# Sums of q and k's seven products kept in PSUM, and the last pair of tiles by seven products too

## The chip, the cores and the metric

The kernel runs on one NeuronCore of a Trainium2 chip. The metric is the device time of one execution in microseconds (us); lower is better. The engines named below are TensorE (PE, matmuls; its weight loads are PEld), VectorE (DVE), ScalarE (ACT), GpSimd (POOL) and SyncE (SP, whose queue issues most DMAs). PSUM is the memory that matmuls write; it has eight banks of 512 float32 columns for each partition, and GpSimd doesn't read it.

## What is computed

One transformer-like block on x of 2048 rows and 512 columns, in float32: a layer norm, then a sliding dilated attention beside a feed-forward with squared ReLU, whose SiLU gates the attention's output.

```python
xn = _layernorm(x, axis=-1)
s = _A_ref(xn, A_wqkv, A_wo)      # 32 heads of 16; each row attends to 8 rows, 2 apart
g = _silu(_B_ref(xn, B_w1, B_b1, B_w2, B_b2))
return x + s * g

# in _A_ref
qkv = (x @ wqkv).reshape(B, S, 3, H, Dh)
...
# in _B_ref, F = 1792
h = x @ w1 + b1
h = where(h > 0, h, 0) ** 2
out = h @ w2 + b2
```

## The kernel before

**Precision.** Each matmul operand is split into a high part (rounded to the type that TensorE multiplies fast) and a low part (the rest). A product of two operands is three passes: high by high, high by low, low by high (`PASSES`). One matmul is 128 x 128 by 128 x 512 and fills a bank. `split` makes both parts: ScalarE copies the high one, VectorE or GpSimd subtracts for the low one.

**Stage one** (`px`, `pstg`, `pxT` pools): the 2048 rows are 16 tiles of 128, handled in pairs (a, a + 1). For each tile, q, k and v come from xn times three 512 x 512 weights, 12 matmuls each (four pieces of 128 of the contraction, three passes; `qkv`). ScalarE evacuates each bank into a staging tile `stg` (four buffers), which is stored to HBM in the layout of the attention (`store_qkv`, in SP's queue), from where it is loaded again, unit by unit, by DMAs that ScalarE issues (`load_u`).

A pair can be done in two ways. `pair` does six `qkv`, 72 matmuls. `pair_of_seven` treats the q and k of a pair as a 2 x 2 block product: the two tiles by the two halves of the contraction, times the two halves of the weights of q (Q0, Q1) and of k (K0, K1). It takes seven products of six matmuls in place of eight (the form of Strassen's scheme due to Winograd), 42 matmuls and 24 for v. With sums S of x's quarters (made by `copy_quarter`, `sums`, `high_sums`, `low_sums` beside the pair before) and sums T1 to T4 of the weights:

- P1 = x(a, half 0) Q0, P2 = x(a, half 1) Q1, P5 = S1 T1, P6 = S2 T2, P7 = S3 T3, P3 = S4 K1, P4 = x(b, half 1) T4
- U2 = P1 + P6, U3 = U2 + P7
- q of a = P1 + P2; k of a = U2 + P5 + P3; q of b = U3 + P4; k of b = U3 + P5

Before, `SEVEN` holds the pairs 4, 6, 8, 10 and 12; pairs 0, 2 and 14 are plain. Each product goes to a bank of its own (`psA`, four banks in rotation, of which v's products take theirs too). ScalarE copies P1 and P5 into q's and k's staging tiles; VectorE does five additions of 128 x 512, each reading a bank, and GpSimd two.

**The order** is written by hand. `Ordered` keeps every engine's instructions in program order. `beside(a, step)` is called at six points of each pair and runs what `plan` puts there for the next pairs (transposes, splits of x, the sums S, layer norms, shuffles), takes in feed-forward weights (`next_w`, where `ahead` says so), and calls `pump`, which lets VectorE's attention work run on as far as a planned clock allows: `clock["V"]` to at most `LATE` = 3000 ns past `clock["PE"]`. `not_before` sets VectorE's planned clock to when an input is due.

**Stage two**: four chunks of 512 rows, each with 14 slices of the feed-forward (`up`, 12 matmuls into `psH`, then ScalarE and GpSimd; `down`, 12 matmuls into four banks of `psA`), the attention's output product, and the gate. Slices 0 and 1 of the first chunk are computed within pair 14, as `last`.

**Weights' homes**: the split weights of qkv and the sums T1 to T4 fill ten buffers, of which `HOME` says which feed-forward slice takes which buffer over once the old content is used. There are 14 slices; slices 0 to 4 are split during stage one, at steps (10, 2), (12, 4), (14, 0), (14, 2) and (14, 4).

The records of the trace have the line of a helper (L87) for every engine instruction, so groups are told apart by tile names: `pm` the products of a seven-product pair, `pq` the plain ones, `ph` and `pb` the feed-forward's up and down, `S` and `Sf` the sums of x.

Of the kernel before, what the change touches and what calls it, by code (L numbers as in the profile page):

```python
# [8 lines left out]
F32 = mybir.dt.float32  # L9
# [5 lines left out]
P = 128  # L15
# [25 lines left out]
HOME = {0: 10, 1: T1, 2: T2, 3: T3, 4: T4, 5: Q0, 6: Q1, 7: K0, 8: K1, 9: V0, 10: V1}  # L41

SEVEN = range(4, 14, 2)
# [14 lines left out]
def body(ctx: ExitStack, tc: tile.TileContext, x, wqkv, wo, w1, b1, w2, b2, out):  # L58
# [52 lines left out]
    def psA(name):  # L111
        return psum.tile([P, 512], F32, name=name, tag="acc", bufs=4)
# [421 lines left out]
    def product(a, n, lhs, w):  # L534

        ps = psA(f"pm{a}_{n}")
        k = 0
        for i in range(2):
            for p, q in PASSES:
                PE.matmul(ps, lhs(p, i), wq[w][:, q, i, :], start=k == 0, stop=k == 5)  # L540
                k += 1
        return ps.rearrange("p (g c) -> p g c", g=GR)
# [4 lines left out]
    def qkv(t, s, between=None, late=False):  # L547
# [5 lines left out]
        for n, (kt, a, b) in enumerate(order):  # L553
            PE.matmul(ps, xt[t][:, a, kt], wq[2 * s + kt // 2][:, b, kt % 2, :], start=n == 0, stop=n == 11)
            if between and n == 5:
                between()
# [196 lines left out]
    def pair_of_seven(a):  # L753
# [39 lines left out]
        qkv(b, 2)  # L793
# [213 lines left out]
```

## Time and profile before

| | |
|---|---|
| median of three runs | 496.27 us (492.69 to 496.73) |
| span of the profiled execution, first to last instruction | 487.2 us |
| matmuls and transposes on TensorE | 2124 |
| ScalarE, GpSimd busy | 220.0 us, 242.7 us |
| stage one, from the first matmul on x to the first `up` | 6.92 to 127.00 us |

The time of a run is that of the whole execution on the device. The span counts from the first to the last instruction of the program; what lies around it is the difference, some 9 us between the median and the span of the profiled execution.

In the rows below, a row of the timeline reads: start us, length us, engine, line, operation, out<-in, shapes, count, and in brackets the engine's idle time before it and what ended that. A row of the groups reads: line, engine, operation, out<-in, shapes, count, then busy us, mean ns of one, idle time before them and what ended it. A row of the chain reads: start us, length us, what. A row of the stretches reads: from:to, length, then busy us (and instructions) of PE, PEld, DVE, ACT and POOL, the granted clock, the DMA share and GB/s. The slices are 40 equal parts of the span, each digit the busy share in tenths, 9 for 90% or more.

### The profile page before, as it was taken

The numbers are of one execution on the slowest core, as the hardware profiler recorded it, in microseconds if no ns is written. First come the engines' busy times: TensorE is split into PE (matmuls) and PEld (weight loads), VectorE is DVE, ScalarE is ACT, GpSimd is POOL, SyncE is SP. The second block draws the span as 40 slices with busy tenths as digits, with TensorE's granted clock in tenths as the row PEclk, the third lists the DMA queues.
The fourth block names the chain that finished last, engine by engine and source line by source line (L and its number), as shares of the span: only waits on it lengthen the run. The fifth ranks groups of instructions, "written<-read, shape, count | busy, mean of one in ns | idle before, by whom it ended". The sixth has DMA issues, their size and how long they took to land.

```text
span 487.2 us, 5957 instructions
## 1 busy us (share of the span) xinstructions
PE 481.0 (99%) x2124; PEld 395.4 (81%) x2124; DVE 437.9 (90%) x369; ACT 220.0 (45%) x392; POOL 242.7 (50%) x178
## 2 busy tenths in 40 slices
PE   8999999999999999999999999999999999999996
PEld 5887788888888888888888888888888888888886
DVE  5987999999999997999999999999999999989234
ACT  5556386523454657336612432652233366223331
POOL 1325244044657869367546426784643488352210
PEclk9999999999999999999999999999999999999999
DMA  8899999879938998274618337371924755030322
GB/s 281 219 249 278 302 289 278 215 210 315 289 87 221 264 194 229 77 233 76 170 45 209 82 64 262 60 200 31 226 48 85 248 93 152 16 108 23 86 86 88
DMA packets 65530, 81.47 MB, mean 167 GB/s; under 512 B 6108, under 2 KB 49372, under 8 KB 64732
## 3 DMA queue, kind: packets, MB, share of 16 engines
q1 hardware_dynamic: 61180, 54.87, 40.6%
q10 hardware_dynamic: 4320, 26.22, 21.3%
q8 instruction: 17, 0.28, 0.3%
q14 instruction: 13, 0.11, 0.1%
HBM read 50.60 MB, written 27.32 MB: 160 GB/s over the span
## 4 chain that ended last, share of the span: by engine, by line
PE 96%; DVE 1%; issue 1%; DMA 1%; POOL 0%; ACT 0%; POOLq 0%
PE pb L87 31%; PE ph L87 31%; PE pq L87 15%; PE pm L87 9%; PE pw L87 9%; DVE pr L87 1%; DMA x<-in_A_x 1%; PE pxT L87 0%; POOL stg L87 0%; DVE z L87 0%; ACT xn L87 0%; DVE Sf L87 0%; DVE st L87 0%; ACT S L87 0%; DVE stg L87 0%
## 5 line engine op out<-in xcount | busy, mean ns | idle before, releaser
L87 PE MATMUL pb<-w,h 128*128 128x512 f32 x672 | 160.6, 389 | 0.0
L87 PEld LDWEIGHTS pb<-w,h 128*128 128x128 f32 x672 | 126.1, 188 | 26.2
L87 POOL TENSOR_TENSOR h<-hf,h 128x512 fp32r<-128x512 f32 x46 | 83.8, 1822 | 104.4 <-ACT hf L87 95.3
L87 PE MATMUL ph<-xU,w 128*128 128x512 f32 x504 | 120.6, 389 | 0.0
L87 PEld LDWEIGHTS ph<-xU,w 128*128 128x128 f32 x504 | 94.6, 188 | 19.6
L87 ACT ACTIVATE ph<-ph,b1t 128x512 f32<-128x512 f32 x56 | 36.9, 659 | 136.8 <-PE ph L87 135.5
L87 DVE TENSOR_TENSOR pr<-k,q 128x2048 f32<-128x2048 f32 x32 | 81.4, 2543 | 0.6
L87 DVE TENSOR_TENSOR pv<-v,L 128x2048 f32<-128x2048 f32 x32 | 79.0, 2468 | 2.5 <-POOL L L87 2.0
L87 DVE TENSOR_REDUCE L<-pr 128x128 f32<-128x2048 f32 x32 | 73.2, 2286 | 0.9
L87 DVE TENSOR_REDUCE v<-pv 128x256 f32<-128x2048 f32 x32 | 73.0, 2281 | 0.8
L87 PE MATMUL pw<-wot,oT 128*128 128x512 f32 (+1 forms) x204 | 45.9, 376 | 0.0
L87 PE MATMUL pq<-wq,xt 128*128 128x512 f32 x192 | 45.5, 389 | 0.0
L87 PEld LDWEIGHTS pw<-wot,oT 128*128 128x128 f32 x204 | 36.8, 188 | 7.1
L87 PEld LDWEIGHTS pq<-wq,xt 128*128 128x128 f32 x192 | 36.0, 188 | 7.5
L87 PE MATMUL ph<-xT,w 128*128 128x512 f32 x168 | 40.3, 389 | 0.0
L87 PEld LDWEIGHTS ph<-xT,w 128*128 128x128 f32 x168 | 31.5, 188 | 6.5
L87 ACT ACTIVATE h<-ph 128x512 fp32r<-128x512 f32 x56 | 33.7, 601 | 1.8
L87 ACT ACTIVATE stg<-pq 128x512 f32<-128x512 f32 x28 | 16.6, 597 | 39.5 <-PE pq L87 39.5
L87 POOL TENSOR_TENSOR w<-w1r,w 128x512 fp32r<-128x512 f32 x14 | 25.6, 1830 | 16.0 <-ACT w L87 15.6
L87 ACT ACTIVATE hf<-ph 128x512 f32<-128x512 f32 x46 | 27.3, 594 | 8.9 <-POOL h L87 8.9
L87 PE MATMUL pq<-wq,xT 128*128 128x512 f32 x132 | 30.9, 393 | 0.0
L87 PE MATMUL pm<-wq,S 128*128 128x512 f32 x120 | 29.7, 394 | 0.3 <-ACT S L87 0.3
(82 smaller groups left out, 505.1 us busy)
## 6 DMA issues: line engine op xcount, KB each, us to landing
k<-sk ACTq DMA_DIRECT2D x8, 960.0 KB, 7.9
v<-sv ACTq DMA_DIRECT2D x8, 960.0 KB, 8.2
sx<-xt SPq DMA_DIRECT2D x12, 512.0 KB, 5.6
xU<-sx ACTq DMA_DIRECT2D x6, 1024.0 KB, 7.9
x<-in_A_x SPq DMA_DIRECT2D x16, 256.0 KB, 5.2
sk<-stg SPq DMA_DIRECT2D x8, 512.0 KB, 4.9
sq<-stg SPq DMA_DIRECT2D x8, 512.0 KB, 5.7
sv<-stg SPq DMA_DIRECT2D x8, 512.0 KB, 5.7
```

The source lines that it names most:

```text
L87: return tc.keep_in_program_order(f(*a, **k))
```

## The change

1. The sums of the seven products are built in the banks themselves. Three banks are held through a pair: `sums_ps`, `first` and `five`. P1 goes to `sums_ps`; ScalarE copies that bank into the bank `first`. P6 is then accumulated onto `sums_ps` (U2), P2 onto `first` (q of a), P7 onto `sums_ps` (U3), P4 onto `sums_ps` (q of b), and P3 onto `five`, which held P5. ScalarE copies each stage out when it is needed: P5, U2 (into a new tile `u2`), q of a, U3, q of b. Of VectorE's five additions one is left (k of a = u2 + `five`), of GpSimd's two one (k of b).
2. The order of a pair changes: the v of the first tile comes after P1 and P5, and P7 and P3 are put into the middle of the second tile's v (`seventh`, run after its sixth matmul). Steps 3 and 4 of `beside` come six matmuls later in the pair, and the store of q is the pair's last.
3. `SEVEN` takes in pair 14, in place of its 48 matmuls for q and k. The sums S are then made for pair 14 too.
4. `HOME` is permuted: slice 1 takes K0's buffer (which has no further use once all later pairs are by seven), slices 2, 3 and 4 those of T1, T2 and T3, slice 7 that of K1, slice 8 that of T4.

```diff
-HOME = {0: 10, 1: T1, 2: T2, 3: T3, 4: T4, 5: Q0, 6: Q1, 7: K0, 8: K1, 9: V0, 10: V1}
-SEVEN = range(4, 14, 2)
+HOME = {0: 10, 1: K0, 2: T1, 3: T2, 4: T3, 5: Q0, 6: Q1, 7: K1, 8: T4, 9: V0, 10: V1}
+SEVEN = range(4, 16, 2)
...
-    def product(a, n, lhs, w):
-        ps = psA(f"pm{a}_{n}")
+    def product(ps, lhs, w, start=True):
         k = 0
         for i in range(2):
             for p, q in PASSES:
-                PE.matmul(ps, lhs(p, i), wq[w][:, q, i, :], start=k == 0, stop=k == 5)
+                PE.matmul(ps, lhs(p, i), wq[w][:, q, i, :], start=start and k == 0, stop=k == 5,
+                          skip_group_check=True)
                 k += 1
...
-        p = product(a, 1, part_x(a, 0), Q0)
-        A.activation(q[:, :, 0], p, AF.Copy)
-        p = product(a, 5, part_s(a, 0), T1)
-        A.activation(k[:, :, 1], p, AF.Copy)
+        sums_ps, first, five = (psA(f"pm{a}_{n}") for n in range(3))
+        u2 = pstg.tile([P, GR, CH], F32, name=f"u2_{a}", tag="u2")
+        product(sums_ps, part_x(a, 0), Q0)
+        A.activation(first, sums_ps, AF.Copy)
+        product(five, part_s(a, 0), T1)
+        A.activation(k[:, :, 1], heads(five), AF.Copy)
         beside(a, 0)
-        p = product(a, 6, part_s(a, 1), T2)
-        not_before(clock["PE"])
-        V.tensor_add(k[:, :, 0], q[:, :, 0], p)
-        p = product(a, 2, part_x(a, 1), Q1)
+        qkv(a, 2)
         beside(a, 1)
-        not_before(clock["PE"])
-        V.tensor_add(q[:, :, 0], q[:, :, 0], p)
-        p = product(a, 7, part_s(a, 2), T3)
-        not_before(clock["PE"])
-        V.tensor_add(q[:, :, 1], k[:, :, 0], p)
-        G.tensor_add(k[:, :, 0], k[:, :, 0], k[:, :, 1])
-        G.tensor_add(k[:, :, 1], k[:, :, 1], q[:, :, 1])
-        p = product(a, 3, part_s(a, 3), K1)
+        product(sums_ps, part_s(a, 1), T2, False)
+        A.activation(u2, heads(sums_ps), AF.Copy)
+        product(first, part_x(a, 1), Q1, False)
+        A.activation(q[:, :, 0], heads(first), AF.Copy)
         beside(a, 2)
-        qkv(a, 2)
-        not_before(clock["PE"] - 12 * MATMUL)
-        V.tensor_add(k[:, :, 0], k[:, :, 0], p)
-        store_qkv(b, 1)
-        beside(a, 3)
-        p = product(a, 4, part_x(b, 1), T4)
-        beside(a, 4)
-        not_before(clock["PE"])
-        V.tensor_add(q[:, :, 1], q[:, :, 1], p)
-        store_qkv(b, 0)
+
+        def seventh():
+            product(sums_ps, part_s(a, 2), T3, False)
+            A.activation(q[:, :, 1], heads(sums_ps), AF.Copy)
+            G.tensor_add(k[:, :, 1], k[:, :, 1], q[:, :, 1])
+            product(five, part_s(a, 3), K1, False)
+            not_before(clock["PE"])
+            V.tensor_add(k[:, :, 0], u2, heads(five))
+            store_qkv(b, 1)
+            beside(a, 3)
+
         if last:
             for f in range(2):
                 up(0, f)
                 pump()
             lowh(0)
-        qkv(b, 2)
+        qkv(b, 2, seventh)
+        beside(a, 4)
+        product(sums_ps, part_x(b, 1), T4, False)
+        A.activation(q[:, :, 1], heads(sums_ps), AF.Copy)
+        store_qkv(b, 0)
         beside(a, 5)
```

`heads(ps)` is the view of a bank by head groups that `product` returned before.

More of the change, by code (lines that the diff above doesn't have):

```diff
@@ L539, in product, with heads @@
             for p, q in PASSES:
-                PE.matmul(ps, lhs(p, i), wq[w][:, q, i, :], start=k == 0, stop=k == 5)
+                PE.matmul(ps, lhs(p, i), wq[w][:, q, i, :], start=start and k == 0, stop=k == 5,
+                          skip_group_check=True)
                 k += 1
+    def heads(ps):
         return ps.rearrange("p (g c) -> p g c", g=GR)
@@ L553, in qkv @@
         for n, (kt, a, b) in enumerate(order):
-            PE.matmul(ps, xt[t][:, a, kt], wq[2 * s + kt // 2][:, b, kt % 2, :], start=n == 0, stop=n == 11)
+            PE.matmul(ps, xt[t][:, a, kt], wq[2 * s + kt // 2][:, b, kt % 2, :], start=n == 0, stop=n == 11,
+                      skip_group_check=True)
             if between and n == 5:
```

## The prediction

> **What bounds the kernel now.** I read the page first (busy times, slices, chain), then the chain in order of time, then TensorE's own timeline.
>
> ```profile
> span 487.2 us, 5957 instructions
> PE 481.0 (99%) x2124; PEld 395.4 (81%) x2124; DVE 437.9 (90%) x369; ACT 220.0 (45%) x392; POOL 242.7 (50%) x178
> DVE  5987999999999997999999999999999999989234
> PEclk9999999999999999999999999999999999999999
> PE 96%; DVE 1%; issue 1%; DMA 1%; POOL 0%; ACT 0%; POOLq 0%
> ```
>
> TensorE is busy 99% and carries 96% of the chain that ended last, at the full granted clock in every slice. VectorE is 90% busy, but its last three slices are nearly empty, so its work has room and TensorE's has none. A busy matmul row proves no pace, since matmuls overlap; the chain in order of time gives the pace.
>
> ```profile
> 42.26 7.35 PE pm L87 x31
> 73.95 8.16 PE pm L87 x36
> 88.92 8.16 PE pm L87 x36
> 103.88 8.16 PE pm L87 x36
> 116.11 10.88 PE pq L87 x48
> ```
>
> 36 matmuls take 8.16 us, 0.2267 us each, and so do the 48 in 10.88 us. Pairs 8 and 10 of the seven-product kind run from 73.95 to 103.88: 29.93 us for 2 x 66 matmuls, which is 132 x 0.2267 and nothing else. Pairs 4 and 6 run from 42.26 to 73.95: 31.69 us for the same 132. So all waiting of TensorE there is 31.69 - 29.93 = 1.76 us, and most of it is at one seam:
>
> ```profile
> 57.43 0.61 PE L87 MATMUL pm<-wq,xt 128*128 128x512 f32 x2
> 58.23 1.20 PE L87 MATMUL pm<-wq,xt 128*128 128x512 f32 x4 [0.19 <-DVE xt L87]
> 59.69 3.31 PE L87 MATMUL pm<-wq,S 128*128 128x512 f32 x12 [0.25 <-ACT S L87]
> ```
>
> Pair 6 begins at 57.43 and waits for VectorE's low part of x and for ScalarE's copy of the sums S, which VectorE makes late. At full pace those first six would have ended at 57.43 + 1.36 = 58.79; the twelve start at 59.69, so 0.90 us are lost, and more on the twelve's first matmuls.
>
> **The change, part by part.**
>
> *Pair 14 by seven products.* Plain: 6 x 12 = 72 matmuls. Seven products: 7 x 6 + 24 for v = 66. Six fewer at 0.2267: **-1.36 us**, all on TensorE, which is the path.
>
> In the Trainium skill, "TensorE: Matmul & The Clock Gate", section "Wait — 56ns, not 53.3ns?", a warm matmul of 512 columns starts 215.7 ns after the last; by that, six would be an estimated 1.29 us. The trace's 226.7 ns decides.
>
> *VectorE's, ScalarE's and GpSimd's load.*
>
> ```profile
> L87 DVE TENSOR_TENSOR stg<-stg,pm 128x512 f32<-128x512 f32 x25 | 16.7, 682 | 4.3 <-PE pm L87 1.4 <-POOL stg L87 1.1 <-DMA sk<-stg 0.9
> L87 DVE TENSOR_TENSOR S<-Sf,S 128x512 fp32r<-128x512 f32 x10 | 6.8, 684 | 1.8 <-ACT S L87 1.8
> L87 DVE TENSOR_TENSOR Sf<-pxT,Sf 128x256 f32<-128x256 f32 x10 | 4.2, 421 | 0.2
> L87 ACT ACTIVATE stg<-pm 128x512 f32<-128x512 f32 x10 | 5.8, 593 | 5.4 <-DMA sk<-stg 2.7 <-PE pm L87 1.9 <-DMA w2r<-in_B_w 0.8
> L87 ACT ACTIVATE ph<-ph 128x512 f32<-128x512 f32 x10 | 5.9, 594 | 0.0
> L87 POOL TENSOR_TENSOR stg<-stg 128x512 f32<-128x512 f32 x5 | 6.5, 1292 | 29.4 <-DVE stg L87 22.4 <-ACT mean L87 3.9 <-issue 3.2
> ```
>
> VectorE loses four of five adds in each of five pairs, 20 x 0.682 = 13.6 us, and gains for pair 14 one add, four half sums (0.421) and two low parts (0.684): 3.7 us. Net -9.9 us, worth 0 at the end, as VectorE has idle slices there; it matters only where TensorE waits on it. ScalarE gains four copies in each of five pairs. They cost 0.593 us as the x10 row of stg shows; the new form, PSUM to PSUM, has its nearest row in the 594 ns of ph from ph, so I take 0.594. GpSimd goes from two adds to one (-1.29 us a pair). A matmul that begins a product without clearing its bank does what the later ones of every product do already: 0.
>
> *The new order and its waits.* In matmuls from a pair's start: Q0 to 6, T1 to 12, v of the first tile to 24, T2 to 30, Q1 to 36, half of v of the second tile to 42, T3 to 48, K1 to 54, the other half to 60, T4 to 66. Four products now wait for ScalarE: T2 for the copy of Q0's bank, T3 for u2, T4 for the first copy of q's odd rows, the second tile's v for the fourth bank, which the first tile's v must have left. Covers: T2, 18 matmuls less a copy, 4.08 - 0.59 = 3.49 us; the other three, 12 matmuls less a copy, 2.72 - 0.59 = **2.13 us**. Behind a waiting TensorE stands everything; behind a late ScalarE stand these copies, as its queue is in order. How late is ScalarE now?
>
> ```profile
> 42.09 1.53 PE L87 MATMUL pm<-wq,xt 128*128 128x512 f32 x6
> 44.62 0.58 ACT L87 ACTIVATE stg<-pq 128x512 f32<-128x512 f32 x1
> 47.14 1.06 ACT L87 ACTIVATE stg<-pm 128x512 f32<-128x512 f32 x2
> 75.35 0.60 ACT L87 ACTIVATE stg<-pm 128x512 f32<-128x512 f32 x1
> 90.31 0.60 ACT L87 ACTIVATE stg<-pm 128x512 f32<-128x512 f32 x1
> 108.58 0.60 ACT L87 ACTIVATE stg<-pm 128x512 f32<-128x512 f32 x1 [2.66 <-DMA sk<-stg]
> 60.00:75.00 15.00, 15.00 (x66) 11.93 (x65) 13.87 (x24) 13.44 (x31) 6.55 (x14) 1.00 1.00 299
> ```
>
> Pair 4: Q0 issues from 42.09 to 43.45 and is copied at 47.14, 3.69 us late, over 2.13 but about T2's 3.49 (T2 comes at 42.09 + 24 x 0.2267 = 47.53, the copy ends about 47.7: 0.2 us of wait). Pair 4's first v also wants the bank evacuated at 44.62 to 45.20, and comes at 42.09 + 2.72 = 44.81: 0.4 us. Pairs 8 and 10: copied at 75.35 and 90.31, within 0.1 us of the product's last results. Pair 6 is the doubtful one: ScalarE is busy 13.44 of 15 us and gets 4 x 0.594 = 2.4 us more, 15.8 in 15; but these times overlap (the two copies at 47.14 take 1.06, 0.53 each), so the true load is nearer 14. I take 0.2 us there, between 0 and 0.8. The 2.66 us that ScalarE stood at 108.58 for a store was before its second copy of the pair; in the new order the copy that T2 needs goes ahead of that one, and the first v's evacuation has until matmul 36, so even a repeat is covered: 12 matmuls + 2.66 us + two copies end near matmul 29.
>
> ScalarE's last copy must also wait for GpSimd's add, which reads what it overwrites: 1.29 us after matmul 48's copy, done near matmul 57, wanted at 66. Covered.
>
> *The seams.* Steps 3 and 4 beside a pair, which make the next pair's sums, move six matmuls (1.36 us) later, while the next T1 keeps its place.
>
> ```profile
> 87.07 0.68 DVE L87 TENSOR_TENSOR S<-Sf,S 128x512 fp32r<-128x512 f32 x1
> 90.11 2.20 PE L87 MATMUL pm<-wq,S 128*128 128x512 f32 x9
> 103.46 0.68 DVE L87 TENSOR_TENSOR S<-Sf,S 128x512 fp32r<-128x512 f32 x1
> 105.07 2.88 PE L87 MATMUL pm<-wq,S 128*128 128x512 f32 x12
> L87 DVE TENSOR_REDUCE L<-pr 128x128 f32<-128x2048 f32 x32 | 73.2, 2286 | 0.9
> ```
>
> T1's third matmul is the first to read a low part. Into pair 10 it comes at 90.11 + 0.45 = 90.56, the low part at 87.75: 2.81 us of cover, 1.45 after the move. Into pair 12: 105.52 against 104.14, 1.38, leaving 0.02. Against the move stand the adds that VectorE no longer has in front of these parts: it runs at most 3000 ns ahead by the planner's bound, and the plan puts the pair's only add at matmul 54 with nothing as long as a product between it and the low part. So I take 0 at these seams (bounds: -0.7, one add gone, to +2.3, one long reduction in front). At the seam into pair 6 the same thinning takes away most of the old loss: I keep 0.3 of 0.9.
>
> *The rest.*
>
> ```profile
> L87 POOL TENSOR_TENSOR w<-w1r,w 128x512 fp32r<-128x512 f32 x14 | 25.6, 1830 | 16.0 <-ACT w L87 15.6 <-DMA w2r<-in_B_w 0.4
> L87 POOL TENSOR_TENSOR w<-w2r,w 128x512 fp32r<-128x512 f32 x14 | 22.6, 1614 | 0.0
> L87 ACT ACTIVATE w<-w1r 128x512 fp32r<-128x512 f32 x14 | 8.8, 628 | 9.0 <-DMA w1r<-in_B_w 9.0
> 108.60 0.53 ACTq L87 DMA_DIRECT2D k<-sk  x1
> 109.17 1.00 ACTq L87 DMA_DIRECT2D q<-sq  x1
> ```
>
> The weights' new homes: w2, w3 and w4 take the buffers of T1, T2 and T3 in steps that follow each buffer's last product, so ScalarE finds them free. A split is two copies and two subtractions, 2 x 0.63 + 1.83 + 1.61 = 4.7 us. The last, w4's, has 54 matmuls (T4, two of up, two of down: 12.2 us) before its first use: 0, and up to 4.7 us, once, if that cover were gone. ScalarE also issues the attention's loads, 1.53 us for a k and a q: under the 2.13 us of cover where one falls in front of a copy. The k store moves six matmuls later and the q store twelve; both wait in SP's queue ahead of the next pair's spill and shuffle, which are read a pair (15 us) later: 0.
>
> **Sum**, against the profiled execution: -1.36 - 1.76 + (0.2 + 0.4 + 0.2 + 0.3 and some 0.1 of restarts) = **-1.9 us**, span 485.3. The median of the three runs, 496.27, is 9.1 above the span; nothing outside the span changes, so 496.3 - 1.9 = **494.4 us**.
>
> **Rivals.**
>
> 1. *Only the matmuls count* (18%): the seam into pair 6 and pair 4's waits stay as they are, and new small waits cancel what goes: 496.3 - 1.4 = 494.9, or up to 496.3 with 1.4 us of new waits.
> 2. *The sums come late at every seam* (9%), the slower side: VectorE's stream fills the freed time with a reduction just before the low part. It decides once cover is under one such operation (2.29 us, from the row shown with the seams); covers left are 1.45 and 0.02, so on average about 1.6 us at each of five seams, 8.0, and 0.1 each to restart: 487.2 - 3.1 + 8.5 = 492.6, 501.7 us. For it: 0.02 us at one seam, and a planner that fills all it may. Against: 13.6 us of adds gone.
> 3. *ScalarE's queue becomes the loop* (6%): if copies run 3.69 us late, as in pair 4, at a step with 2.13 us of cover in each of six pairs, 6 x 1.56 = 9.4: span 493.5, 502.6 us. Against it: punctual copies in pairs 8 and 10.
> 4. *Small waits halve the clock* (1%): if TensorE's micro-waits between products made one six-matmul product per pair run at half pace, 2.72 us for 1.36, then 6 x 1.36 = 8.2 us: 487.2 - 3.1 + 8.2 = 492.3, 501.4 us. Against it: 0.9 us lost at 57 to 60 and the clock row stayed at 9.
> 5. *Something outside the span shrinks* (4%), faster than TensorE's waits allow, under 491.3.
>
> Rival 4 is what the Trainium skill says in "TensorE: Matmul & The Clock Gate", section "A second HAM failure mode: psum-queue depth-cycling": cycling through PSUM banks can make TensorE idle briefly often enough for its clock gate to oscillate. This trace, with 35 products of seven-product pairs through four banks and the clock row at 9, shows no such thing.
>
> **How the numbers follow.** The forecast has 62%, at 494.4; with all old waits gone and no new ones, 493.2. A change under 1%, 5.0 us, cannot be told from none here, as the three runs lie 4 us apart. Faster by more than that (under 491.3) needs rival 5 or a low reading: 5%. Slower (over 501.2) is rivals 2, 3 and 4: 16%. The rest, 79%, is within. The range: 493.2 less most of the runs' spread, 490.5, to half of rival 2 or 3, 499.5.
>
> **What would show it.** Right: 2118 matmuls, pairs 14.96 us apart from pair 6 on, waits of TensorE under 1.5 us in the stage, VectorE's adds on stg 6 instead of 25. Wrong: TensorE's weight loads waiting for ScalarE's copies of pm (rival 3), or for S at each pair's seventh matmul (rival 2), or a clock row below 9 (rival 4). The forecast falls if those waits add up to over 3 us.

## The result and the profile after

| | before | after |
|---|---|---|
| median of 22 runs each | 492.69 us (488.57 to 496.73) | 494.05 us (491.42 to 499.02) |
| ratio of the times | | **1.0052** [1.0027, 1.0077] |
| span of the profiled execution | 487.2 us | 489.7 us (time 491.57 us) |
| granted clock of the profiled execution | 1.000 | 0.996 |

The medians are of all 22 runs each; the ratio is an estimate from the fast runs alone, with its 95% interval, so it isn't the quotient of the two medians (1.0028).

The change makes the kernel slower by half a per cent. It is a small loss, but its interval doesn't contain 1, and it has the other sign than the forecast of -1.9 us.

The page of the changed kernel, busy times, three rows of the slices, and the chain's shares by engine:

```profile
span 489.7 us, 5949 instructions
...
PE 481.4 (98%) x2118; PEld 395.1 (81%) x2118; DVE 426.5 (87%) x356; ACT 233.0 (48%) x417; POOL 232.3 (47%) x174
...
DVE  5978858987789699996999999699999999999744
...
PEclk9999999999999999998999999999999999999999
...
PE 89%; DVE 4%; issue 3%; POOL 1%; ACT 1%; DMA 1%; ACTq 0%; POOLq 0%; DVEq 0%
```

The work did what the diff says: 2118 matmuls, VectorE 11.4 us less busy, ScalarE 13.0 us more. But TensorE's part of the chain fell from 96% to 89%, VectorE's last three slices, nearly empty before, are less empty (7, 4, 4 for 2, 3, 4), and one slice, the nineteenth (220 to 232 us), has a clock under 9. So the attention ends later although VectorE has less to do, and something happens at 220 us, in stage two, which the prediction never looked at.

TensorE's waits in the changed kernel, longest first (us in total, times, longest; the rows left out belong to the start and were there before):

```profile
PE pb L87 <- POOL h L87: 1.9, 1, 1.9
...
PE pm L87 <- DVE xt L87: 0.5, 1, 0.5
PE pm L87 <- ACT S L87: 0.2, 1, 0.2
```

The first row is new. Its place is the seam between the first and the second chunk of stage two. First the kernel before there, in the timelines of TensorE, ScalarE, GpSimd, SP's queue and VectorE (rows of these five, in order of time):

```profile
207.05 0.55 SPq L323 DMA_DIRECT2D so<-v  x1
...
208.43 5.60 PE L87 MATMUL pb<-w,h 128*128 128x512 f32 x24
...
212.92 0.55 ACTq L87 DMA_DIRECT2D v<-sv  x1
213.52 2.07 ACT L87 ACTIVATE z<-pb 128x512 f32<-128x512 f32 x4 [7.66 <-PE pb L87]
...
220.83 2.29 DVE L87 TENSOR_REDUCE L<-pr 128x128 f32<-128x2048 f32 x1
221.90 1.29 POOL L87 TENSOR_TENSOR h<-hf,h 128x512 fp32r<-128x512 f32 x1
...
224.75 2.88 PE L87 MATMUL pb<-w,h 128*128 128x512 f32 x12
```

and the changed kernel at the same place:

```profile
210.51 0.55 SPq L323 DMA_DIRECT2D so<-v  x1
...
214.30 0.53 ACTq L87 DMA_DIRECT2D v<-sv  x1
214.88 2.06 ACT L87 ACTIVATE z<-pb 128x512 f32<-128x512 f32 x4 [10.23 <-issue]
215.61 7.11 POOL L87 TENSOR_TENSOR z<-z,b2t 128x512 f32<-128x512 f32 x4 [0.85 <-POOL L L87]
...
221.41 3.45 DVE L87 TENSOR_TENSOR pr<-k,q 128x2048 f32<-128x2048 f32 x1
222.67 3.31 POOL L87 TENSOR_TENSOR h<-hf,h 128x512 fp32r<-128x512 f32 x1
223.55 0.61 PE L87 MATMUL pb<-w,h 128*128 128x512 f32 x2
226.04 4.14 PE L87 MATMUL pb<-w,h 128*128 128x512 f32 x10 [1.87 <-POOL h L87]
```

Read it from the top. The attention's result for a unit (v) is stored by `so<-v`; ScalarE's queue then issues the next load of v, which waits until that store has landed, and behind it in the same queue stand the four evacuations of `down`'s banks (z). GpSimd adds a bias to the four z and then makes the low part of h, which the next chunk's first `down` needs from its third matmul on.

The load holds the z in both kernels. Where no load stands in front of them (`v_later_stg5`, below), the first z starts 3.60 us after the 24 matmuls of `down` begin, at 211.29 after 207.69. By that the z could start at 212.03 before and at 210.83 after; they start at 213.52 and 214.88, each just behind the load, though the row of the kernel before names TensorE. After, the store goes out 3.46 us later and the load 1.38 us later, and GpSimd begins its work on the z 1.36 us later (215.61 for 214.25).

Three things together turn this into a stop. TensorE wants the low part at 224.00 instead of 225.21, 1.20 us earlier. The low part starts 0.77 us later, at 222.67 for 221.90. And it takes 2.02 us longer, 3.31 us for 1.29. Before, it lay beside a reduction of VectorE. After, a multiplication of VectorE with two inputs had begun 1.26 us ahead of it, and the low part ends at 225.98, 1.12 us after that multiplication (224.86), about its own time, as if it had waited for it. So where it was there 2.02 us early (223.19), it is 1.98 us late; TensorE's third matmul starts at 226.04, after an idle time of 1.87 us. With its usual 1.29 us the low part would have ended at 223.96, just in time.

And that is half of the price. The stretches around it (from:to, length, busy us of PE, PEld, DVE, ACT, POOL, then granted clock, DMA share, GB/s):

```profile
224.00:226.00 2.00, 0.17 (x1) 0.00 (x0) 0.86 (x1) 0.00 (x0) 1.98 (x1) 1.00 0.00 0
226.00:230.00 4.00, 3.96 (x10) 3.13 (x11) 1.41 (x2) 3.95 (x6) 1.27 (x1) 0.57 0.02 4
```

After the stop the clock is 0.57 for 4 us: ten matmuls fill 226.04 to 230.02, 3.98 us for what takes 2.27 us. With the wait, the stop costs 3.74 us in all. The Trainium skill, "TensorE: Matmul & The Clock Gate", section "What's actually happening", says that the clock is granted by activity in a free-running window of about 3.4 us and falls to half after an idle window; the halving is what this trace shows, but after 1.87 us idle, not 3.4.

The difference of the two profiled spans can now be closed. I count each kernel from pair 4's first matmul (42.09 before, 41.70 after), and call lost every step between two matmuls' starts beyond 0.227 us, behind that point:

| us | before | after | difference |
|---|---|---|---|
| pair 4 begins | 42.09 | 41.70 | -0.39 |
| lost in stage one | 1.58 | 2.18 | +0.60 |
| lost in stage two | 0 | 3.74 | +3.74 |
| the rest: matmuls at full pace, and the end | 443.50 | 442.07 | -1.43 |
| span | 487.18 | 489.69 | +2.51 |

The six matmuls brought what they should (6 x 0.2267 = 1.36), and one stop in stage two took more. This closes the account of two executions, each faster than the median of its kernel: the one after took 491.57 us, and the one before, with the same 1.9 us around its span, some 489.1.

Why is the attention late? VectorE takes its instructions in the order of the program, and the attention is fed to it a bit at a time. Three places of its timeline, first before, then after:

```profile
109.20 2.29 DVE L87 TENSOR_TENSOR pv<-v,L 128x2048 f32<-128x2048 f32 x1
...
135.32 2.29 DVE L87 TENSOR_TENSOR pr<-k,q 128x2048 f32<-128x2048 f32 x1
...
204.74 2.29 DVE L87 TENSOR_REDUCE v<-pv 128x256 f32<-128x2048 f32 x1
```

```profile
96.97 2.28 DVE L87 TENSOR_TENSOR pv<-v,L 128x2048 f32<-128x2048 f32 x1
...
136.88 0.69 DVE L87 TENSOR_TENSOR stg<-u,pm 128x512 f32<-128x512 f32 x1 [5.42 <-PE pm L87]
137.48 2.28 DVE L87 TENSOR_TENSOR pr<-k,q 128x2048 f32<-128x2048 f32 x1
...
208.20 2.29 DVE L87 TENSOR_REDUCE v<-pv 128x256 f32<-128x2048 f32 x1
```

Counting the large operations of the attention (128x2048), the ninth ran at 109.20 before and at 96.97 after, so the additions saved did come through as 12 us of lead. The seventeenth, 135.32 before, is at 137.48 after: in pair 14 VectorE stands 5.42 us at its one addition, which waits for the product K1, and the order puts the 24 matmuls of `up` (126.99 to 132.43 on TensorE) in front of T3 and K1. The lead is gone and 2 us more. By the thirty-third operation the attention is 9.3 us behind (190.23 for 180.90), of which a wait of VectorE for a load of q, 3.37 us at 164.35, is a part; the fortieth, the last before the store at the seam, is 3.46 us late. So the wait in pair 14 is one source of the lateness and not all of it. What the lateness does at the seam can be tested.

### The profile page after: what moved, and what is told of

The parts are those of the page before. It is cut to its first block, busy times and chain, and to the rows that moved or that the text cites. A ratio compares the mean times of both kernels' runs of the same rounds, so it can differ in the third digit from the quotient of the medians.

```text
span 489.7 us, 5949 instructions
## 1 busy us (share of the span) xinstructions
PE 481.4 (98%) x2118; PEld 395.1 (81%) x2118; DVE 426.5 (87%) x356; ACT 233.0 (48%) x417; POOL 232.3 (47%) x174
## 4 chain that ended last, share of the span: by engine, by line
PE 89%; DVE 4%; issue 3%; POOL 1%; ACT 1%; DMA 1%; ACTq 0%; POOLq 0%; DVEq 0%
PE pb L87 28%; PE ph L87 28%; PE pq L87 13%; PE pm L87 11%; PE pw L87 8%; DVE v L87 1%; DVE pv L87 1%; POOL h L87 1%; POOL z L87 1%; DMA x<-in_A_x 1%; DVE L L87 0%; PE pxT L87 0%; ACT z L87 0%; ACT ph L87 0%; ACT w L87 0%
## 5 line engine op out<-in xcount | busy, mean ns | idle before, releaser
L87 PE MATMUL pb<-w,h 128*128 128x512 f32 x672 | 162.5, 392 | 1.9 <-POOL h L87 1.9
L87 POOL TENSOR_TENSOR h<-hf,h 128x512 fp32r<-128x512 f32 x46 | 78.7, 1712 | 101.5 <-ACT hf L87 92.9
L87 DVE TENSOR_TENSOR pv<-v,L 128x2048 f32<-128x2048 f32 x32 | 77.4, 2419 | 2.0 <-POOL L L87 1.2
L87 POOL TENSOR_TENSOR w<-w1r,w 128x512 fp32r<-128x512 f32 x14 | 22.5, 1608 | 33.0 <-ACT w L87 33.0
L87 PE MATMUL pm<-wq,S 128*128 128x512 f32 x144 | 36.2, 392 | 0.2 <-ACT S L87 0.2
L87 PE MATMUL pq<-wq,xt 128*128 128x512 f32 x144 | 35.8, 390 | 0.0
L87 ACT ACTIVATE hf<-ph 128x512 f32<-128x512 f32 x46 | 27.4, 595 | 11.4 <-POOL h L87 11.4
L87 PEld LDWEIGHTS pm<-wq,S 128*128 128x128 f32 x144 | 26.7, 188 | 7.1 <-ACT S L87 0.7
L87 PEld LDWEIGHTS pq<-wq,xt 128*128 128x128 f32 x144 | 26.9, 188 | 6.2 <-ACT stg L87 0.6
```

Of the source, the lines that this page charges most:

```text
L87: return tc.keep_in_program_order(f(*a, **k))
```

## The experiments

The theory (late attention): the change leaves the attention late in stage two; the v load on ScalarE's queue passes that on to the z and to GpSimd's low part of h, and TensorE stops at a seam. Its rivals: ScalarE's new copies hold TensorE in stage one (the prediction's rival 3); or GpSimd's z are too slow by themselves; or pair 14's rearrangement costs by itself. Each ratio is to the kernel before. The expected ranges held for `stg5` (theory A's), `v_later_stg5`, `before_v_later_stg5` and `before_late`; the ratios of the other ten lie outside every range written down for them.

**The two halves of the change alone.** `seven_alone` puts the new `SEVEN` and `HOME` into the kernel before, with the old sums; `sums_alone` keeps the changed sums and takes the old `SEVEN` and `HOME`.

```diff
-HOME = {0: 10, 1: K0, 2: T1, 3: T2, 4: T3, 5: Q0, 6: Q1, 7: K1, 8: T4, 9: V0, 10: V1}
-SEVEN = range(4, 16, 2)
+HOME = {0: 10, 1: T1, 2: T2, 3: T3, 4: T4, 5: Q0, 6: Q1, 7: K0, 8: K1, 9: V0, 10: V1}
+SEVEN = range(4, 14, 2)
```

> Only pair 14 by seven products and the weights' new homes, with VectorE's additions as they were. TensorE does 2118 matmuls. Theory A: TensorE loses no more in stage one than before (1.6 us), comes to the first seam 1.4 us earlier, where the kernel before had 1.56 us of cover, so 0.990 to 1.000 according to what VectorE's extra work in pair 14 does to the attention's place. Theory B: all of the loss is in the sums, so this part alone is a clean gain of 1.4 us, ratio 0.997.

> Only the sums in PSUM and the new order of a pair: pairs 4 to 12 by seven products as before, pair 14 plain, weights' homes as before. TensorE does 2124 matmuls. Theory A: stage one loses about 2 us of TensorE as before (1.6) and after (2.2), there is no wait of 5 us of VectorE in pair 14, and the seams decide: ratio 0.998 to 1.004. Theory B (copies in TensorE's loop cost): ratio 1.005 to 1.010, six matmuls (1.4 us) worse than the whole change.

`seven_alone`: 494.13 us, 1.0046 [1.0010, 1.0081]. `sums_alone`: 496.84 us, 1.0109 [1.0058, 1.0161]. Each half loses, and the two together lose no more than the first. In `seven_alone` the stop is at the same seam and longer, 3.88 us, with its v load as late as 217.94, and the low part of h again takes 3.31 us, behind a multiplication of VectorE that began 1.24 us earlier. In `sums_alone` it sits at the next seam; ScalarE's timeline there, and TensorE's:

```profile
297.88 0.35 ACTq L87 DMA_DIRECT2D xU<-sx  x1
298.28 0.66 ACT L87 ACTIVATE ph<-ph,b1t 128x512 f32<-128x512 f32 x1 [6.79 <-DMA so<-v]
...
308.73 5.49 PE L87 MATMUL ph<-xU,w 128*128 128x512 f32 x23 [2.75 <-issue]
```

ScalarE stood 6.79 us until a store of v had landed, and behind it in the queue was the load of xU, the next chunk's input, for which TensorE stops 2.75 us. So a store of v holds the queue here too, with another victim. The fortieth operation of the attention runs at 211.83 in `seven_alone` and at 205.75 in `sums_alone`, 7.1 and 1.0 us later than before: in these two profiles the lateness at the first seam comes with pair 14 by seven. `sums_alone` also loses 3.45 us in stage one, for 1.58 before, 0.97 of it where ScalarE waits for a staging buffer (see the next test). Neither half is free, and their losses don't add.

**The v load on another queue.** `v_on_sp` lets SP's queue issue the v loads of all units but the first.

```diff
-        A.dma_start(t.rearrange("p i c -> p (i c)"), ap)
+        if what == "v" and u:
+            queue(t.rearrange("p i c -> p (i c)"), ap)
+        else:
+            A.dma_start(t.rearrange("p i c -> p (i c)"), ap)
```

> The changed kernel, with the attention's v loads (all but the first) issued from SyncE's queue in place of ScalarE's. Theory A (the loss is TensorE's stop at the seam between chunks 0 and 1 of stage two, where ScalarE stood in its queue for the v load until 214.30 us and so drained the down banks about 2 us late): the stop of 1.87 us and the 427 ns matmuls after it go, TensorE loses under 0.5 us after 130 us, the span is 486 us, the ratio to the kernel before 0.990 to 0.998. Theory B (stage one's waits for ScalarE's copies are the loss): nothing in stage two matters much, ratio 1.003 to 1.007 as for the change itself. Theory C (GpSimd's own slow additions at that seam are enough): the stop stays at 1 us or more though the v load is out of the way.

494.40 us (488.20 to 496.40), 1.0013 [0.9967, 1.0059]. In the profiled execution (span 487.6 us) the z start 3.60 us after `down`, with no load in front of them, and stage two loses nothing. But stage one loses 3.91 us now, where ScalarE stands longer for the store that frees a staging buffer (in the changed kernel the same wait was 3.72 us, at 110.86):

```profile
112.58 0.60 ACT L87 ACTIVATE stg<-pq 128x512 f32<-128x512 f32 x1 [5.17 <-DMA sk<-stg]
```

TensorE then stands idle 1.02 us for that copy. The same happens in the profiles of `sums_alone`, `v_later`, `z_late` and `early` (ScalarE 5.1 to 5.2 us, TensorE 0.93 to 1.04 us), and in none with a fifth staging buffer: a cost of the new order that the profiled execution of the changed kernel escaped.

The profiled execution agrees with the theory for stage two, narrowly, as the next test shows. The interval does not, since the twelve executions fall into two groups, 488.2 to 489.9 at a clock of 0.999 or more, and 494.4 to 496.4 at 0.992 to 0.997: in seven of them something still stopped TensorE long enough to halve its clock. The profiled execution is not one of them; the next test has one that is.

**The v load later, and a fifth staging buffer.** `v_later` keeps the queue and has the plan issue v loads 9 us, not 2, past VectorE's planned time, so that the store has long landed. `stg5` gives the staging tiles a fifth buffer. `v_later_stg5` does both.

```diff
+FREE_V = 9000
...
-                defer(max(clock["V"] + FREE if u else 0, done_tiles[n][1][u] + LAND), start)
+                defer(max(clock["V"] + (FREE_V if n == "v" else FREE) if u else 0, done_tiles[n][1][u] + LAND), start)
...
-        stgs[s] = pstg.tile([P, GR, 2, CH], F32, name=f"stg{t}_{s}", tag="stg", bufs=4)
+        stgs[s] = pstg.tile([P, GR, 2, CH], F32, name=f"stg{t}_{s}", tag="stg", bufs=5)
```

> The changed kernel, with each v load (all but the first) put off by 7000 ns of the planned clock, still in ScalarE's queue: by then the store before it has landed, so ScalarE need not stand. Theory A (ScalarE held by the v load at the first seam makes GpSimd's low part of h late and TensorE stop, and the halved clock doubles it): TensorE loses under 0.5 us after 130 us, the profiled span is 484 to 488 us, the granted clock of most executions is back at 0.998 or over (the changed kernel: 0.993 to 0.997 in all, the kernel before: 0.998 or over in most), ratio 0.990 to 0.998. Theory C (GpSimd's additions alone): the stop stays, clock under 0.998 in most.

> The changed kernel with a fifth staging buffer alone; the v loads stay where they were. If the staging wait in pair 12 is the root (theory D), ScalarE no longer stands there, the attention comes to the first seam 1 to 2 us earlier, and most of the loss goes: ratio 0.995 to 1.000. If the v load at the seam is the root (theory A), the last reduction before that load still ends near 207 to 209 us, ScalarE is still held at the seam, and the ratio is 1.001 to 1.005.

> As v_later, and a fifth staging buffer. Theory D (beside A: in the new order the first tile's v takes the staging tile that held the k of the pair before, whose store lands only 8 to 10 us after it is issued, so that ScalarE stands 3.7 to 5.2 us in pair 12 and TensorE up to 1.4): that wait in pair 12 goes, stage one loses under 2 us, ratio up to 0.003 below that of v_later, 0.988 to 0.996. If D is wrong, the same as v_later.

| | median us | ratio |
|---|---|---|
| `v_later` | 492.69 | 1.0010 [0.9963, 1.0056] |
| `stg5` | 492.79 | 1.0026 [0.9988, 1.0064] |
| both | 488.09 (487.61 to 493.54) | **0.9940** [0.9896, 0.9985] |

`stg5` alone takes the wait of ScalarE in stage one away and leaves the stop at the seam, 1.88 us at 228.28; its clock was 0.997 or less in all twelve executions. With both, the first seam reads, on ScalarE and TensorE:

```profile
211.29 2.64 ACT L88 ACTIVATE z<-pb 128x512 f32<-128x512 f32 x4 [6.18 <-PE pb L88]
...
224.01 2.88 PE L88 MATMUL pb<-w,h 128*128 128x512 f32 x12
...
225.62 0.54 ACTq L88 DMA_DIRECT2D v<-sv  x1
```

The z wait for TensorE alone, the load goes out behind the seam, the twelve matmuls run through; stage two loses nothing and stage one 2.39 us. This is faster than both kernels, though three of its twelve executions (492.8 to 493.5 us) still show a clock of 0.995 to 0.997.

`v_later` alone has its z free as well, and yet its profiled execution (clock 0.992) stops 1.15 and 3.50 us at two seams. At the second, GpSimd's z stand behind a softmax operation that waited for VectorE until 306.55, though ScalarE had begun to evacuate at 301.00: late attention reaches GpSimd without the v load. At the first seam nothing differs from the version with both but some nanoseconds. VectorE's multiplication and GpSimd's low part of h, first in `v_later_stg5`, then in `v_later`:

```profile
222.29 3.45 DVE L88 TENSOR_TENSOR pr<-k,q 128x2048 f32<-128x2048 f32 x1
222.30 1.29 POOL L88 TENSOR_TENSOR h<-hf,h 128x512 fp32r<-128x512 f32 x1
...
223.53 2.29 DVE L88 TENSOR_TENSOR pr<-k,q 128x2048 f32<-128x2048 f32 x1
223.55 3.39 POOL L88 TENSOR_TENSOR h<-hf,h 128x512 fp32r<-128x512 f32 x1
```

The two begin 11 ns apart in the first and 16 ns apart in the second. In the first, GpSimd takes its usual time and VectorE 3.45 us; in the second, VectorE takes its usual time and GpSimd 3.39 us, and TensorE stops. `v_on_sp` shows a third such tie, 11 ns, which GpSimd wins. So getting the load out of the way doesn't remove the hazard: it turns a meeting that GpSimd loses, 1.26 us behind, into a tie that can go either way. The share of executions at a clock of 0.998 or more fits that, none of 22 for the change, 5 of 12 for `v_on_sp`, 6 of 12 for `v_later`, 9 of 12 for both edits; but only the profiled executions show which way it went.

**The control.** Is that a cure of what the change did, or a gain that the kernel before would have had as well? `before_v_later` and `before_v_later_stg5` make the same edits in the kernel before.

> The control: the kernel before with the same putting off of the v loads. Theory A says that the kernel before meets the seams with 1.4 to 1.6 us of cover, so it gains little: ratio 0.996 to 1.001, clock as before. If this gains as much as v_later does over the changed kernel, the v load was a loss of both kernels and doesn't explain the difference.

> Control: the kernel before with the later v loads and a fifth staging buffer. In its order the v of a pair came later after the last pair's stores, and its one staging wait (2.66 us in pair 12) cost TensorE nothing, so by theory D the fifth buffer changes nothing: ratio 0.991 to 0.996, within 0.003 of the kernel before with the later loads alone (0.993).

488.57 us, 0.9930 [0.9895, 0.9966], and 488.44 us, 0.9923 [0.9889, 0.9956]: as good as the changed kernel with the same edits (0.9940). The hazard at the seam is the old kernel's too: of the 23 executions of it that ran beside the last control, 7 show a granted clock of 0.997 or less, while the kernel before with later loads, in either version, shows 0.998 or more in all of its executions. By the clock, the change made an occasional stop a constant one: 0.993 to 0.997 in all 22 executions. What the later loads shorten in the kernel before is not shown. Its profiled execution loses nothing in stage two without them, the three profiled spans are 487.2, 485.9 and 486.6 us, and at the first seam the load still stands in front of the z (they start at 212.36 in `before_v_later`, 1.56 us later than `down` would allow); at the other two it no longer does.

**GpSimd's z out of the way.** `z_late` puts the four bias additions behind the low parts of h for the next chunk's first two slices.

```diff
             A.activation(z, pb[j], AF.Copy)
-            G.tensor_add(z, z, b2t)
...
             for j in range(TPC):
+                G.tensor_add(gs[c, j], gs[c, j], b2t)
+            for j in range(TPC):
                 silu(c, j)
```

> The changed kernel, with GpSimd's four additions of b2 at a seam put behind the low parts of h of the next chunk's first two slices. Theory A: GpSimd then waits only for ScalarE's h, which is still late by the v load (some 2 us), but is rid of 7 us of additions in front of it, so TensorE does not stop at the down of the next chunk's slice 0; the silu and what follows come later, which may move a smaller wait to the third slice. Ratio 0.990 to 0.999, clock 0.998 or over in most. Theory B (stage one): ratio stays at 1.003 to 1.007.

493.07 us, 1.0018 [0.9982, 1.0054]. The stop at the first `down` is gone: the low part, which now comes before VectorE's multiplication, takes 1.29 us and ends at 223.30 for a matmul at 225.52. But TensorE now waits at the slice behind, in each of three seams:

```profile
234.75 3.02 PE L87 MATMUL ph<-xU,w 128*128 128x512 f32 x12 [0.91 <-ACT hf L87]
```

and 1.83 us at 323.9 and at 413.1. GpSimd's work at the seam is a real part of the chain, but moving it moves the wait, as what comes behind is as tight.

**What in pair 14 makes the attention late.** `ups_late` takes the 24 matmuls of `up` out from in front of T3 and K1, which the addition waits for: they come after the second tile's v.

```diff
+        qkv(b, 2, seventh)
         if last:
             for f in range(2):
                 up(0, f)
                 pump()
             lowh(0)
-        qkv(b, 2, seventh)
```

> The changed kernel, with slices 0 and 1 of the first chunk's up moved behind the second tile's v (and its seventh product) in pair 14, so that VectorE's one addition no longer waits for 24 matmuls of up. Theory A with its root in VectorE's order (the attention lost its lead of some 10 us in pair 14 and after, and so met the seam at another point): VectorE's wait of 5.4 us before that addition goes, the attention runs 4 to 6 us earlier than in the changed kernel from 140 us on, and the wait at the first seam changes; if the seam is met well, ratio 0.990 to 0.998, if not, still 1.002 to 1.006. Theory B: ratio unchanged at 1.003 to 1.007 and the stage-two stop, if any, makes no difference.

496.78 us, 1.0112 [1.0057, 1.0167]: worse. The slices' own h is then late (0.57 and 0.86 us at 162.4 and 169.0), and stops of 2.12 and 1.82 us appear at the second and third seam. It doesn't isolate the wait; it replaces it.

`early` lets the planner put attention work into VectorE's wait, ahead of that addition:

```diff
             product(five, part_s(a, 3), K1, False)
+            if last:
+                pump(LATE)
             not_before(clock["PE"])
             V.tensor_add(k[:, :, 0], u2, heads(five))
```

> The changed kernel with one more call of the attention's pump in pair 14, just before VectorE's addition there, so that the attention works in the 5.4 us in which VectorE stood. Theory E (the jump in VectorE's plan in pair 14 is the cause: it puts the attention's loads and GpSimd's work late at the seams): the attention is 4 to 7 us earlier than in the changed kernel from 160 us on, TensorE loses under 1 us at the seams, ratio 0.992 to 1.000 (6 matmuls gained, stage one's waits as in the change), clock 0.998 or over in most. Theory F (the place of the attention is chance, and the staging wait and the copies in stage one are the cause): ratio 1.002 to 1.007.

496.74 us, 1.0105 [1.0051, 1.0160]: worse too, and yet it did what it should at its place. The seventeenth operation ran at 132.7 and the thirty-third at 180.8, as in the kernel before (180.9; 190.2 after). Then it lost everything in one place, which ScalarE's and VectorE's timelines show:

```profile
196.41 0.63 ACT L87 ACTIVATE w<-w1r 128x512 fp32r<-128x512 f32 x1 [6.01 <-DMA w1r<-in_B_w]
...
198.27 1.29 DVE L87 TENSOR_TENSOR oT<-pT,oT 128x512 fp32r<-128x512 f32 x2 [7.15 <-ACT oT L87]
```

ScalarE's queue waited 6.01 us for a feed-forward weight's DMA, VectorE behind it 7.15 us, so the fortieth operation came 2 us later than in the changed kernel, and TensorE stopped 1.96, 2.21 and 1.82 us in stage two. Why that DMA landed so late (the loads of k and q were issued beside it) was not settled.

`early_v_stg5` adds the later v loads and the fifth buffer to it.

> The changed kernel with all three: the extra pump, the later v loads, a fifth staging buffer. Theory E: ratio 0.988 to 0.994, the lowest of all versions, by the 1.4 us of six matmuls under the kernel before with the later loads (0.993). If not under 0.993, the six matmuls are given back in stage one's waits.

491.41 us (487.44 to 494.44), 0.9979 [0.9937, 1.0021]. No stop in stage two, clock 0.998 or more in all executions; but nothing more is gained over `v_later_stg5`, the interval contains 1, and stage one loses 2.36 us.

`seam6` starts from `v_later_stg5` and makes pair 6's sums a step earlier, to end the waits at stage one's seam.

```diff
-        at(a, n + 2, lowx, t)
+        at(a, n + 1 if n else n + 2, lowx, t)
...
-            at(a, n + 2, sums, t, 0)
+            at(a, n + 1 if n else n + 2, sums, t, 0)
```

> The changed kernel with later v loads, a fifth staging buffer, and, for the pair after pair 4 alone, the low part of x and the first half sums one step earlier beside pair 4. The waits into pair 6 (0.63, 0.42 and some 0.4 us of restarts, 1.4 us in all) should fall below 0.6: ratio 0.991 to 0.994. If VectorE only does the same later elsewhere, the same as without it, 0.994.

499.66 us, 1.0151 [1.0090, 1.0212]. It did what it was for: stage one loses 0.07 us, not 2.39. And it is the slowest of all, because the attention is then 8 us later (its fortieth operation at 216.5, 208.7 in `v_later_stg5`; the ninth already at 106.2, for 97.7), and with the v loads out of the way TensorE stops for the attention's own output. Its waits, by what it waited for:

```profile
PE pw L88 <- DVE oT L88: 8.2, 3, 4.5
```

The 2.3 us won in stage one come back as 8.2 us of waiting and a halved clock behind it.

**Late attention alone.** The last test leaves the change out altogether. `before_late` is the kernel before, where the planned clock of VectorE is set 5.4 us forward once, in pair 14: no instruction is added or taken away, the attention is only handed out later.

```diff
         if last:
             lowh(0)
+            clock["V"] += 5400
         qkv(b, 2)
```

> The kernel before, with VectorE's planned clock put forward by 5400 ns once, in pair 14; nothing else is changed, and no instruction is added or taken away. Theory E: the attention falls 4 to 9 us behind as in the changed kernel, the first seam finds ScalarE at the v load, ratio 1.003 to 1.012, clock under 0.998 in most. Theory F: ratio 0.998 to 1.002.

494.99 us, 1.0049 [1.0014, 1.0084], against the change's 1.0052 [1.0027, 1.0077]. At the seam of the first two chunks, ScalarE's queue and TensorE:

```profile
217.60 0.55 ACTq L87 DMA_DIRECT2D v<-sv  x1
...
221.99 3.02 PE L87 MATMUL ph<-xU,w 128*128 128x512 f32 x12 [0.87 <-ACT hf L87]
...
229.42 4.63 PE L87 MATMUL pb<-w,h 128*128 128x512 f32 x10 [3.95 <-POOL h L87]
```

and the clock by stretches:

```profile
226.00:230.00 4.00, 0.58 (x1) 0.50 (x2) 1.03 (x1) 0.60 (x1) 3.36 (x2) 0.78 0.06 16
230.00:236.00 6.00, 6.00 (x17) 4.71 (x16) 4.00 (x3) 5.10 (x8) 2.04 (x2) 0.58 0.00 0
```

A late load again (217.60), the same waiting for GpSimd's low part of h, the same half clock behind it, without one of the change's copies or products. It is no copy of the change: its attention is 3.1 us later at this point than the changed kernel's (the fortieth operation at 211.3), the stop in the profiled execution is longer, and it is GpSimd's work on the four z that takes long here (9.21 us for 7.11), while the low part takes 1.25. But lateness alone is enough to make such a loss.

## Why the prediction went wrong

Point by point, by its own steps:

- **Six matmuls, -1.36 us: right.** The row of the rest fell by 1.43 us, and the seven-product pairs still follow one another at 14.96 us where nothing waits: in the changed kernel's chain T4 of a pair, with the next Q0 and T1 behind it, begins at 87.46 and again at 102.42.

- **The old waits, -1.76, for new ones of +1.2: mis-sized.** Stage one lost 0.60 us more than before, where the sum had 0.56 less. Pair 4's waits did not come in this profile (its twelve-matmul steps run through at 44.42 and 47.22), but the seam into pair 6, where I kept 0.3 of 0.9, loses about 1.8. The timeline of TensorE and the chain there:

```profile
55.38 1.98 PE L87 MATMUL pm<-wq,xt 128*128 128x512 f32 x8
57.82 1.20 PE L87 MATMUL pm<-wq,xt 128*128 128x512 f32 x4 [0.47 <-DVE xt L87]
59.27 1.92 PE L87 MATMUL pm<-wq,S 128*128 128x512 f32 x6 [0.25 <-ACT S L87]
61.21 3.02 PE L87 MATMUL pq<-wq,xt 128*128 128x512 f32 x12
```

```profile
54.98 2.20 DVE L L87
57.17 0.59 DVE xt L87
```

  At the pace of 0.2267 us the rows should start at 57.19, 58.73 and 60.63; they start 0.63, 0.54 and 0.58 us late. In front of the low part of x (xt) stands a reduction of 2.20 us: the planner filled the freed room with attention. That is rival 2's mechanism, at one seam of five, where the prediction gave a thinner stream the credit. ScalarE's wait for a store in pair 12, which the prediction called covered even if it came again, cost TensorE some 0.2 us here and an idle time of 0.93 to 1.04 us in five other profiles of the new order.
- **ScalarE's copies: right in size.** They took 0.595 us into staging tiles and 0.583 us from bank to bank (forecast 0.594):

```profile
L87 ACT ACTIVATE stg<-pm 128x512 f32<-128x512 f32 x24 | 14.3, 595 | 9.4 <-PE pm L87 9.3
...
L87 ACT ACTIVATE pm<-pm 128x512 f32<-128x512 f32 x6 | 3.5, 583 | 0.8 <-PE pm L87 0.7
```

  In this profile they mostly wait for TensorE and not the other way round: weight loads of `pm` and `pq` waited 1.1 us for them in all. Rival 3, ScalarE late in every pair, did not occur; ScalarE late in pair 12 alone did, in the five profiles just named.
- **"Net -9.9 us, worth 0 at the end, as VectorE has idle slices there": the step that failed.** The load fell (by 11.4 us), but the load was not what counted. The step went on "it matters only where TensorE waits on it" and looked for such places in stage one alone. The removal of the additions gave the attention a lead of 12 us, which was gone by the seventeenth operation, and the fortieth came 3.46 us late. At the seam behind it GpSimd's low part of h had been there 2.02 us before TensorE wanted it; now it came 1.98 us too late. Half of these 4.0 us came from its meeting with a multiplication of VectorE. That is +3.74 us in the profiled execution. The part on the rest of the change followed SP's and ScalarE's queues within stage one, and the covers of stage two's seams were never counted.
- **Rival 4, the halved clock: right in kind, wrong in place.** Its sign, a clock row below 9, is there in one slice, but no chain of small waits did it; one stop of 1.87 us was followed by a half clock that cost 1.71 us more.
- **Rival 1** (only the matmuls count, the seam into pair 6 stays): nearest for stage one; with nothing in stage two it would have been a gain.
- **"9.1 us lie around the span": misread.** The profiled run of the changed kernel took 491.57 us for a span of 489.69: 1.9 us lie around it. The median run before simply had a longer span. The forecast of 494.4 is so close to the 494.05 measured because its base, three runs with a median of 496.27, was 3.6 us above the 22 runs' 492.69; that is chance. "Within 1%" holds, the forecast's direction doesn't.

Shown: in the profiled execution the loss is one stop in stage two, where TensorE waits for GpSimd's low part of h; and late attention alone makes such a loss (`before_late`). Not shown is the share of each route by which lateness gets there. The traces show three, the v load in ScalarE's queue, the softmax operation in GpSimd's, and the meeting of GpSimd with VectorE's multiplication; in the changed kernel's stop the third is the largest, 2.02 us, and no run removes it alone. What the change is worth with later loads and a fifth buffer on both sides is about nothing: 0.9940 [0.9896, 0.9985] against 0.9923 [0.9889, 0.9956], intervals that overlap widely. In the profiles of these two, stage one loses 2.39 us with the change and 1.30 without, which takes most of the 1.36 us of the six matmuls back. Three things stay open: the late weight DMA in `early`, what the later loads gain in the kernel before, and why single executions at a clock of 1.000 still differ by some us (pair 4 began between 41.7 and 43.9 us in the profiled executions of these kernels, which explains 2 of them).

## What to carry to other kernels

Work taken off an engine that isn't the bound can still move its other work later, when what is left on that engine waits in order for something new: follow the first and last operation that others depend on into the next stage, and count the cover at each seam there, in time and on each in-order queue. A load that waits for a store, on the queue of an engine that evacuates TensorE's banks, holds the evacuations up, by 1.4 to 1.5 us at each of the three seams in the profile of the kernel before; issuing the loads some us later made that kernel 0.7% faster. Price GpSimd's operations twice, alone and beside a two-input operation of VectorE. And when an edit moves an old hazard, run the cure on the kernel before as well, or the cure's gain is credited to the change.

## What the runs showed of the hardware

**How long a stop halves the clock is not fixed.** Half pace (0.427 us for a matmul) followed idle times of TensorE of 1.87, 1.88, 1.96, 2.21 and 2.48 us, and all four of 3.5 us and more; it did not follow 1.82, 1.83, 2.12 and, in `sums_alone`, 2.75 us, where the clock was 1.000 over the whole span. Between some 1.9 and 2.8 us it falls out either way. The free-running window that the Trainium skill has in "TensorE: Matmul & The Clock Gate", section "What's actually happening", fits that, for the phase then decides; an idle time as long as its window, 3.4 us, was not needed. After each stop that halved it, the granted clock stayed at half for 3.41 or 6.83 us, one or two such windows. Half pace lasted 7 to 14 matmuls.

**GpSimd beside VectorE.** An addition or subtraction of 128x512 takes GpSimd 1.29 us alone or beside VectorE's reductions. When a multiplication of two inputs by VectorE has begun over 20 ns before, it ends 1.1 to 1.3 us after that multiplication and so takes up to 3.4 us, as in the changed kernel's stop. When the two begin within 20 ns of each other, either can win: the winner takes its usual time (GpSimd 1.29 us, VectorE 2.29), and the loser as much longer as it has to wait (VectorE 3.45, GpSimd 3.4). The Trainium skill, "SBUF — State Buffer", section "SBUF: two separate sides", says that of a VectorE instruction with two SBUF inputs and one of GpSimd whichever starts first gets a shared port pair for the whole instruction, and the other waits; the trace agrees. Of the ten stops of over 1 us that TensorE made for the low part of h in the profiles of these runs, eight have a low part of 3.3 to 3.4 us: on such a seam, which of VectorE's operations comes at that time is worth 2 us.
